# A matmul kernel whose hand-written opening list is written anew, with sixteen idle matmuls of the identity in it

## The chip, the cores and the metric

The kernel runs on one core of a Trainium2 chip. The metric is the device time of one launch in microseconds (us); less is better. The kernel before took 530.66, 531.22 and 532.54 us in three runs, median 531.22 us.

## The reference

Two stages follow each other. The first is a recurrence over 768 tokens for 4 batches and 8 heads of 48 channels; the second is a gated feed-forward layer on the 3072 resulting rows of 384.

```python
for t in range(S):
    kt, vt, rt = (k[:, :, t], v[:, :, t], r[:, :, t])
    cur = np.einsum('bhd,bhe->bhde', u[None] * kt, vt)
    y[:, :, t] = np.einsum('bhd,bhde->bhe', rt, state + cur)
    state = w[None, :, :, None] * state + np.einsum('bhd,bhe->bhde', kt, vt)
...
gate = 1.0 / (1.0 + np.exp(-(x @ w_gate)))
val = x @ w_val
return (gate * val @ w_out).astype(np.float32)
```

## The kernel before, in words

The recurrence is cut into 12 chunks of 64 tokens, and each chunk into two groups of heads: 24 groups n. For a group, TensorE makes a table of scores (step Z, line 375), VectorE copies its lower triangle into a zeroed tile (K, line 383), TensorE multiplies that with the values and the queries with the running state (I, line 337) and forms the state's increment (O, line 337 too). ScalarE decays the state (d) and VectorE adds the increment (s). The result is split into a rounded high part (h, ScalarE, line 474) and a low rest (l, VectorE, line 478); both are the rows that the feed-forward layer reads.

The feed-forward layer runs on six tiles of 512 rows with the 1536 inner columns in 12 blocks f. A block's up-projection U is 18 matmuls (line 516): nine for the gate half into one accumulator bank, nine for the value half into another. Then follow a sigmoid (g, ScalarE), a product (m, VectorE), a rounded copy (H, ScalarE), its rest (q) and the down-projection D (line 554). Weights arrive in 64-bit words, and are cast (c), joined (j), rounded (w) and left with a rest (o, or ov on VectorE) before U can use them. For the first row tile the blocks f = 0 and f = 1 run on 256 rows at a time, since its second chunk is ready only later.

Every engine works its instructions off in the order in which they were written. For the first row tile that order is a string, START, of step names: "Z.2" is the score step of group 2, "u.0a" the gate half of block 0 on the first 256 rows. A second, regular loop does the other five tiles. The kernel uses eight accumulator banks: two for scores (sc), three in a rotating pool (ring), three that hold the down-projection's sums (acc0 to acc2). Early on, acc0 also takes four transpositions (step tt, line 197). The identity is made first on GpSimd (masks.py:197 and masks.py:199).

In the working below, "value half" and "gate half" are the two halves of U; the first blocks are U.0 (f = 0) and U.1 (f = 1) on the first 256 rows.

Of the kernel before, what the change touches and what calls it, by code (L numbers as in the profile page):

```python
# [21 lines left out]
P = 128  # L22
# [21 lines left out]
L.0 W.0 L.1 X.0 W.1 L.2 X.1 X.2 tc A.0 tk ti.1 R.0 ti.0 k.0 tp tr Z.0 tt K.0 I.0 c0.0 A.1 c0.1 tn  # L44
h.0 c.1 T.2 T.1 k.1 Rv.1 j0.1 l.0 Tv.0 j0.0 Z.1 O.0 W.2 F.0 W.3 L.3 L.4 W.4 X.3 j.1 K.1 I.1 O.1 A.2
w0.0 sa.0 w.1 h.1 w0.1 o0.1 o.1 R.3 Rv.2 k.2 o0v.0 l.1 s.1 Z.2 K.2 U.0 I.2 O.2 g.0 c.2 d.2 A.3 m.0
U.1 H.0 g.1 h.2 j.2 k.3 s.2 l.2 q.0 T.3 m.1 F.2 L.5 W.8 X.4 L.6 W.5 W.6 L.7 X.5 F.1 X.6 L.8 W.7 Z.3
K.3 I.3 O.3 w.2 A.4 k.4 H.1 c.3 h.3 l.3 R.4 D.0 Z.4 U.2 d.3 s.3 g.2 c.4 j.3 w.3 j.4 qv.1 m.2 o.2
U.4 H.2 g.4 w.4 A.5 K.4 q.2 U.3 D.2 g.3 Rv.5 m.3 k.5 ov.3 m.4 T.4 I.4 O.4 Z.5 H.3 A.6 d.4 h.4 H.4
c.6 c.5 k.6 s.4 K.5 l.4 Tv.5 j.6 R.6 q.3 D.1 D.3 U.5 I.5 g.5 h.5 j.5 qv.4 l.5 m.5 o.4 Z.6 D.4 R.7  # L50
O.5 U.6 A.7 d.5 H.5 K.6 k.7 s.5 q.5 T.6 w.5 ov.5 U.7 c.8 c.7 g.6 j.7 m.6 L.9 X.8 ub Y.8 W.9 W.10
X.7 I.6 Z.7 O.6 D.5 w.6 g.7 ov.6 d.6 w.7 H.6 s.6 j.8 qv.6 h.6 l.6 m.7 w.8 ov.7 H.7 qv.7 D.6 U.8 K.7
R.8 c.9 ov.8 g.8 m.8 Tv.7 H.8 U.9 qv.8 g.9 k.8 j.9 w.9 o.9 m.9 D.7 U.10 g.10 H.9 c.10 j.10 m.10 q.9
D.8 I.7 H.10 d.7 Z.8 O.7 h.7 w.10 D.9 s.7 U.11 ov.10 l.7 W.11 F.5 X.9 F.6 F.3 F.7 F.4 Y.9 qv.10
g.11 c.11 j.11 D.10 U.12 m.11 w.11 R.9 ov.11 U.13 g.12 H.11 qv.11 m.12 H.12 qv.12 g.13 t.8 D.11 b.8
i.8 D.12 K.8 k.9 m.13 H.13 q.13 b.9 T.9 t.9 i.9 T.8
# [4 lines left out]
def rwkv_then_moe(ctx: ExitStack, tc: tile.TileContext, wd, ub, ch, tk, rt, wt, rk0, vn0, wd0, out):  # L61
# [38 lines left out]
    def load_channels(n):  # L100
        c, g = GROUPS[n]
        chan[n] = ach.tile([P, 2, 512], F32, name="chan")
        nc.sync.dma_start(out=chan[n], in_=ch[c, g])

    def load_tokens(n):
        c, g = GROUPS[n]
        toks[n] = atk.tile([P, 2, TKW], F32, name="toks")
        nc.sync.dma_start(out=toks[n], in_=tk[c, g])
# [15 lines left out]
    def constants():  # L124
        make_identity(nc, ident)
        nc.gpsimd.memset(causal, 0.0)
# [7 lines left out]
        for t in score:  # L134
            nc.gpsimd.memset(t, 0.0)
        nc.gpsimd.memset(state, 0.0)
        nc.scalar.activation(table, ident[:, 0:1], AF.Sigmoid)
        nc.vector.memset(tops[0].rearrange("q n two -> q (n two)").bitcast(F32), 0.0)
        nc.gpsimd.memset(tops[1].rearrange("q n two -> q (n two)").bitcast(F32), 0.0)


# [109 lines left out]
    def round_weights(f, c):  # L251
# [3 lines left out]
        nc.scalar.copy(out=whi[f][:, c], in_=w32[f][:, c])  # L255
# [24 lines left out]
    def table_of(n):  # L280
        return tabk[:, 4 * GROUPS[n][1] : 4 * GROUPS[n][1] + 4]
# [8 lines left out]

    def queries(n, eng=nc.gpsimd):
# [210 lines left out]
    class Moe:  # L502
# [3 lines left out]

        def up(self, f):
            w = whi[f], wlo[f]
            self.pair[f] = []
            for g in range(2):  # L510
                o = one_bank()
                self.pair[f].append(o)
                k = 0
                for kt in range(3):
                    for a, b in PASS:
                        nc.tensor.matmul(  # L516
                            o[:, self.cols], w[a][:, g * DM + kt * P : g * DM + (kt + 1) * P],
                            self.x[:, kt, b, self.cols], start=(k == 0), stop=(k == 8),
                        )
                        k += 1  # L520
# [106 lines left out]
    steps = {
        "b": own_tokens, "i": diagonal, "ub": lambda: load_bonus(),
        "N": idle_matmuls,
        "L": load_channels, "X": load_tokens, "Y": load_own, "W": load_weights, "A": bonus_keys, "R": queries, "t": turn_queries,  # L630
        "k": keys, "T": token_keys, "Z": scores, "K": keep, "I": apply, "O": outer,
        "d": decay_state, "s": add_state, "h": x_high, "l": x_low, "F": fills, "D": finish,
        "tc": constants, "tk": channel_table, "ti": inverses, "tp": token_powers,
        "tr": lambda: token_order(nc.vector.tensor_copy), "trA": lambda: token_order(nc.scalar.copy),
        "sa": lambda n: add_state(n, nc.scalar.copy), "tt": token_turn, "tn": token_table,
        "c": lambda f: cast_top(f, ALL), "c0": lambda j: cast_top(0, HALVES[j]),
        "j": lambda f: join_words(f, ALL), "j0": lambda j: join_words(0, HALVES[j]),
        "w": lambda f: round_weights(f, ALL), "w0": lambda j: round_weights(0, HALVES[j]),
        "o": lambda f: rest_of_weights(f, ALL), "o0": lambda j: rest_of_weights(0, HALVES[j]),
# [3 lines left out]
        "qv": lambda i: moe_of(items[i]).h_low(items[i][2], nc.vector),  # L643
        "U": lambda i: moe_of(items[i]).up(items[i][2]),
        "g": lambda i: moe_of(items[i]).sigmoid(items[i][2]),
        "m": lambda i: moe_of(items[i]).product(items[i][2]),
        "H": lambda i: moe_of(items[i]).h_high(items[i][2]),
        "q": lambda i: moe_of(items[i]).h_low(items[i][2]),
# [25 lines left out]
    for i in range(n0, len(items)):  # L674
# [24 lines left out]
        finish(i - 1)  # L699
# [193 lines left out]
```

## Time and profile before

| | us |
|---|---|
| Runs, median (lowest to highest) | 531.22 (530.66 to 532.54) |
| Span of the profiled execution, first to last instruction | 532.9 |
| TensorE busy in it | 510.4 |
| TensorE's first instruction at | 7.63 |
| VectorE, ScalarE, GpSimd busy | 203.4, 186.9, 189.9 |

The page gives no other time of the profiled execution than its span. A busy time is the sum of an engine's stretches of work; the span less that is what the engine stood idle. Stretches of a row in time order begin at the first number and last for the second, and a bracket at the end holds the idle time ahead and what ended it.

### The profile page before, as it was taken

To read this page: it belongs to the slowest core of one execution; us is meant where nothing else is said; L and a number is where in the kernel's file an instruction comes from. 1 tells how busy PE (TensorE), PEld (TensorE's weight loads), DVE (VectorE), ACT (ScalarE), POOL (GpSimd) and SP (SyncE) were. 2 spreads that over 40 slices of the span, in tenths; PEclk is the share of its full clock that TensorE was granted. 3 is DMA by queue.
4 is the path that set the end of the run, shared out by engine and by line. 5 is a ranking of instruction groups with operands and counts; after the bars stand their busy time and mean duration, and the time that the engine had idled before them with its cause. 6 is when DMAs were issued, how large, how long until landed. Compare 5 with 4: busy or idle time off the path is not lost. (4 is left out here: it accounts for less than half of the span.)

```text
span 532.9 us, 11951 instructions
## 1 busy us (share of the span) xinstructions
PE 510.4 (96%) x5204; PEld 424.4 (80%) x5204; DVE 203.4 (38%) x344; ACT 186.9 (35%) x396; POOL 189.9 (36%) x159
## 2 busy tenths in 40 slices
PE   3689999999999999999999999999999999999994
PEld 3678878888888888888888888888888888888883
DVE  8857868464243242341431532431442211111111
ACT  5577665545133233233232331331432222212111
POOL 4362530406453352443452552542253111112210
PEclk9999999999999999999999999999999999999999
DMA  8939736030321230420221420312400000100001
GB/s 321 366 111 352 301 112 284 4 103 21 127 87 26 71 106 1 145 86 17 80 61 48 145 87 0 97 34 72 146 17 2 11 11 10 60 0 1 0 2 64
DMA packets 15723, 47.84 MB, mean 90 GB/s; under 512 B 2384, under 2 KB 5200, under 8 KB 14256
## 3 DMA queue, kind: packets, MB, share of 16 engines
q1 hardware_dynamic: 15664, 47.01, 25.3%
q8 instruction: 43, 0.70, 0.6%
q14 instruction: 16, 0.13, 0.1%
HBM read 39.92 MB, written 4.72 MB: 84 GB/s over the span
## 5 line engine op out<-in xcount | busy, mean ns | idle before, releaser
L516 PE MATMUL ring<-xt,wx 128*128 128x512 f32 (+1 forms) x1332 | 309.9, 387 | 0.9 <-ACT sg L525 0.5
L516 PEld LDWEIGHTS ring<-xt,wx 128*128 128x128 f32 x1332 | 247.8, 191 | 51.3 <-ACT sg L525 0.7
L538 POOL TENSOR_TENSOR h<-sg,h 128x512 fp32r<-128x512 f32 (+1 forms) x66 | 88.5, 1340 | 259.5 <-ACT h L534 259.5
L554 PE MATMUL acc<-h,wx 128*128 128x512 f32 (+1 forms) x666 | 161.6, 388 | 0.4 <-POOLq L714 0.4
L554 PEld LDWEIGHTS acc<-h,wx 128*128 128x128 f32 x666 | 121.2, 188 | 25.6 <-POOLq L714 0.8
L529 DVE TENSOR_TENSOR sg<-ring,sg 128x512 f32<-128x512 f32 (+1 forms) x74 | 50.0, 676 | 237.0 <-PE ring L516 235.6
L525 ACT ACTIVATE sg<-ring 128x512 f32<-128x512 f32 (+1 forms) x74 | 43.4, 586 | 157.4 <-PE ring L516 157.4
L534 ACT CAST h<-sg 128x512 fp32r<-128x512 f32 (+1 forms) x74 | 45.0, 608 | 144.2 <-DVE sg L529 138.2
L293 POOL TENSOR_TENSOR dec<-chan,tabk 128x512 f32<-128x512 f32 x21 | 29.0, 1381 | 12.5 <-PE ring L337 12.4
L478 DVE TENSOR_TENSOR xt<-ring,xt 112x256 fp32r<-112x256 f32 (+1 forms) x52 | 19.9, 418 | 33.1 <-ACT xt L474 33.0
L308 POOL TENSOR_TENSOR toks<-toks,tabn 128x384 f32<-128x384 f32 x19 | 24.0, 1267 | 13.7 <-DMA toks<-in_tk 13.7
L314 POOL TENSOR_TENSOR dec<-dec,toks 128x384 f32<-128x384 f32 x16 | 16.3, 1020 | 27.3 <-DMA dec<-in_rt 27.3
L304 DVE TENSOR_TENSOR chan<-chan,tabk 128x512 f32<-128x512 f32 x24 | 25.0, 1042 | 0.9 <-ACT dec L287 0.9
L375 PE MATMUL sc<-dec,chan 48*64 48x64 f32 x768 | 17.4, 231 | 7.7 <-DVE chan L304 7.6
L383 DVE COPY_PREDICATED score<-masks,sc 128x512 f32<-128x512 int32 x32 | 23.9, 747 | 1.9 <-PE sc L375 1.1
L428 ACT ACTIVATE state<-state,pw 112x96 f32<-112x96 f32 x80 | 23.4, 362 | 2.6 <-PE ring L337 2.6
L337 PE MATMUL ring<-score,toks 64*48 64x64 f32 (+1 forms) x768 | 17.2, 230 | 5.0 <-DVE score L383 4.1
L447 DVE TENSOR_TENSOR state<-state,ring 48x192 f32<-48x192 f32 (+1 forms) x52 | 17.9, 350 | 9.7 <-ACT xt L474 4.7
L375 PEld LDWEIGHTS sc<-dec,chan 48*64 48x64 f32 x768 | 15.0, 145 | 8.1 <-POOL dec L293 7.6
L247 DVE SCALAR_TENSOR_TENSOR wf<-wr,top 128x1152 int32<-128x1152 int32 (+1 forms) x13 | 16.9, 1310 | 9.4 <-ACT top L240 5.7
L337 PEld LDWEIGHTS ring<-score,toks 64*48 64x48 f32 (+1 forms) x768 | 14.6, 137 | 6.4 <-DVE score L383 4.8
L474 ACT CAST xt<-ring 112x256 fp32r<-112x256 f32 (+1 forms) x52 | 16.7, 364 | 7.6 <-PE ring L337 7.3
(60 smaller groups left out, 250.5 us busy)
## 6 DMA issues: line engine op xcount, KB each, us to landing
wr<-in_wt SPq DMA_DIRECT2D x11, 1152.0 KB, 9.2
chan<-in_ch SPq DMA_DIRECT2D x24, 512.0 KB, 4.2
toks<-in_tk SPq DMA_DIRECT2D x24, 400.0 KB, 4.8
out_y<-wf SPq DMA_DIRECT2D x17, 256.0 KB, 2.5
dec<-in_rt SPq DMA_DIRECT2D x16, 192.0 KB, 2.7
xt<-xt SPq DMA_DIRECT2D x30, 64.0 KB, 2.3
wr<-in_wt SPq DMA_DIRECT2D x2, 576.0 KB, 5.4
xt<-xt SPq DMA_DIRECT2D x12, 32.0 KB, 4.2
```

Of the source, the lines that this page charges most:

```text
L293: eng.tensor_tensor(v4(t[:, 0]), v4(chan[n][:, 0]), bc2(table_of(n)[:, :, ::-1]), ALU.mult)
L304: nc.vector.tensor_tensor(v4(k), v4(k), bc2(table_of(n)), ALU.mult)
L308: eng.tensor_tensor(v4(k), v4(k), bc2(tabn[:, 4 * g : 4 * g + 4]), ALU.mult)
L337: nc.tensor.matmul(yb[n][bank][64 * half : 64 * half + m, cs], lhsT, rhs, start=first, stop=stop, skip_group_check=True,)
L375: nc.tensor.matmul(sc[64 * gm : 64 * gm + 64, be, o : o + C], kk[row, cs : cs + C], rr[row, cs : cs + C], start=True, stop=True,)
L383: nc.vector.copy_predicated(t.rearrange("q (b m i) -> q b m i", b=2, m=4), masks[:, m].bitcast(I32).unsqueeze(1).unsqueeze(1).broadcast_to ...
L516: nc.tensor.matmul(o[:, self.cols], w[a][:, g * DM + kt * P : g * DM + (kt + 1) * P], self.x[:, kt, b, self.cols], start=(k == 0), stop=(k ...
L525: nc.scalar.activation(sg[:, c], self.pair[f][0][:, c], AF.Sigmoid, scale=UP)
L529: nc.vector.tensor_tensor(sg[:, c], self.pair.pop(f)[1][:, c], sg[:, c], ALU.mult)
L534: nc.scalar.copy(out=h[:, 0, c], in_=sg[:, c])
L538: eng.tensor_tensor(h[:, 1, c], self.sg.pop(f)[:, c], h[:, 0, c], ALU.subtract)
L554: nc.tensor.matmul(self.acc[d][:, self.cols], w[a][:, 2 * DM + d * P : 2 * DM + (d + 1) * P], h[:, b, self.cols], start=(f == 0 and k == 0 ...
```

## The change

START is written anew. The steps got finer names (a block's gate half u and value half v apart; making the identity, the masks and the zeroed tiles apart), and the string names a few steps in another sequence. As the instructions stand on each engine, this leaves SyncE and GpSimd without any difference, ScalarE with two pairs of neighbours exchanged later on (a rounded copy of h and one of weights), and VectorE with none but a tile's name. TensorE gets idle matmuls: step "N.k" multiplies the identity by itself k times, 128 by 128 in fp32, into the first accumulator bank, and nothing reads the result. There are sixteen at eight places: six ahead of Z.0, two behind I.0, two behind O.0, one behind O.1, two behind Z.2, one between the halves of U.1, one behind Z.3 and one behind O.3. Beside them, the output banks of group 1 come from acc1 and acc2 in place of the rotating three.

```diff
-    def idle_matmuls(k):
-        t = pacc.tile([P, 512], F32, name="acc2")
+        t = accs[0][0] if 0 in accs else pacc.tile([P, 512], F32, name="acc0")
         for _ in range(k):
             nc.tensor.matmul(t[:, 0:P], ident, ident, start=True, stop=True)
...
     def outputs(n):
-        yb[n] = one_bank(), one_bank()
+        if n == 1:
+            yb[n] = tuple(pacc.tile([P, 512], F32, name=f"acc{i}") for i in (1, 2))
+        else:
+            yb[n] = one_bank(), one_bank()
...
-L.0 W.0 L.1 X.0 W.1 L.2 X.1 X.2 tc A.0 tk ti.1 R.0 ti.0 k.0 tp tr Z.0 tt K.0 I.0 c0.0 A.1 c0.1 tn
+ta L.0 tov.0 tc tb W.0 ts.0 L.1 ts.1 X.0 tz W.1 tk L.2 X.1 to.1 N.6 ti.1 X.2 ti.0 A.0 R.0 W.2 k.0
+c0.0 tp tr Z.0 tt A.1 K.0 c0.1 tn k.1 I.0 Rv.1 N.2 j0.1 h.0 l.0 Tv.0 Z.1 c.1 j0.0 O.0 A.2 j.1 w0.0
...
+        def up_one(self, f, g):
+            w, o, k = (whi[f], wlo[f]), one_bank(), 0
+            self.pair.setdefault(f, []).append(o)
+            for kt in range(3):
+                for a, b in PASS:
+                    nc.tensor.matmul(
+                        o[:, self.cols], w[a][:, g * DM + kt * P : g * DM + (kt + 1) * P],
+                        self.x[:, kt, b, self.cols], start=(k == 0), stop=(k == 8),
+                    )
+                    k += 1
```

On TensorE the program begins, before, with the scores of group 0 (sc) and the four transpositions (acc from sg):

```order
L888 UNCONDITIONAL_BRANCH
L375 MATMUL sc<-dec,chan 64x64 x16
L375 MATMUL sc<-chan,dec 64x64 x16
L197 MATMUL acc_201<-spare,sg 128x128 x4
L337 MATMUL ring<-score_97,toks 64x64 x2
```

After the change six idle matmuls (acc from spare, the identity) stand ahead of them:

```order
L921 UNCONDITIONAL_BRANCH
L640 MATMUL acc_151<-spare 128x128 x6
L392 MATMUL sc<-dec,chan 64x64 x16
L392 MATMUL sc<-chan,dec 64x64 x16
L204 MATMUL acc_211<-spare,sg 128x128 x4
L351 MATMUL ring<-score_97,toks 64x64 x2
```

The lines of the kernel shifted (375 is now 392, and so on), and only the six rows are new. Farther on, on TensorE again, before, O.1 ends, then come the scores of group 2 and the 18 matmuls of U.0:

```order
L337 MATMUL ring<-toks 48x48 x2
L375 MATMUL sc<-dec,chan 64x64 x16
L375 MATMUL sc<-chan,dec 64x64 x16
L516 MATMUL ring<-xt,wx 128x256 x18
L337 MATMUL ring<-dec,state 64x64 x2
```

After, one idle matmul stands between O.1 and Z.2 and two between Z.2 and U.0, and O.1 writes to acc1 and acc2:

```order
L351 MATMUL acc_337<-toks 48x48
L351 MATMUL acc_336<-toks 48x48
L640 MATMUL acc_378<-spare 128x128
L392 MATMUL sc<-dec,chan 64x64 x16
L392 MATMUL sc<-chan,dec 64x64 x16
L640 MATMUL acc_420<-spare 128x128 x2
L529 MATMUL ring<-xt,wx 128x256 x18
L351 MATMUL ring<-dec,state 64x64 x2
```

Nothing else moved there. At U.1 and Z.3, before:

```order
L516 MATMUL ring<-xt,wx 128x256 x18
L375 MATMUL sc<-dec,chan 64x64 x16
L375 MATMUL sc<-chan,dec 64x64 x16
L337 MATMUL ring<-dec,state 64x64 x2
```

and after, with one idle matmul between the halves of U.1 and one behind Z.3:

```order
L529 MATMUL ring<-xt,wx 128x256 x9
L640 MATMUL acc_432<-spare 128x128
L529 MATMUL ring<-xt,wx 128x256 x9
L392 MATMUL sc<-dec,chan 64x64 x16
L392 MATMUL sc<-chan,dec 64x64 x16
L640 MATMUL acc_432<-spare 128x128
L351 MATMUL ring<-dec,state 64x64 x2
```

Again the rows between stand as they stood.

## Rows read from the trace of the kernel before

**Rows 1.** The page's first line.

```profile
span 532.9 us, 11951 instructions
```

**Rows 2.** Stretches: length, busy us of each engine (count), granted clock, DMA share.

```profile
0.00:40.00 40.00, 25.53 (x624) 23.08 (x625) 29.34 (x52) 23.49 (x53) 19.57 (x26) 1.00 0.71 266
40.00:100.00 60.00, 58.80 (x830) 49.12 (x832) 43.90 (x61) 37.77 (x70) 18.66 (x12) 1.00 0.60 233
100.00:500.00 400.00, 400.00 (x3656) 331.24 (x3645) 126.32 (x226) 119.81 (x265) 146.43 (x118) 1.00 0.18 56
531.60:532.90 1.30, 0.00 (x0) 0.00 (x0) 0.00 (x0) 0.00 (x0) 0.00 (x0) 0.50 0.03 6
```

**Rows 3.** Instructions in time order, TensorE: start, length, what, idle ahead.

```profile
7.63 1.13 PE L375 MATMUL sc<-dec,chan 48*64 48x64 f32 x32 [7.63 <-DVE chan L304]
...
11.31 1.12 PE L337 MATMUL ring<-score,toks 64*64 64x64 f32 x32 [0.65 <-DVE score L383]
...
17.63 1.12 PE L337 MATMUL ring<-score,toks 64*64 64x64 f32 x32 [2.24 <-DVE score L383]
20.45 0.99 PE L337 MATMUL ring<-toks 64*64 64x48 f32 x30 [1.71 <-POOL toks L308]
...
23.21 0.79 PE L516 MATMUL ring<-xt,wx 128*128 128x256 f32 x2
24.18 3.78 PE L516 MATMUL ring<-xt,wx 128*128 128x256 f32 x16 [0.18 <-DVE xt L478]
27.90 1.12 PE L337 MATMUL ring<-dec,state 48*64 48x64 f32 x32
...
31.18 2.24 PE L516 MATMUL ring<-xt,wx 128*128 128x256 f32 x9
33.89 1.33 PE L516 MATMUL ring<-xt,wx 128*128 128x256 f32 x9 [0.47 <-ACT sg L525]
35.15 0.69 PE L375 MATMUL sc<-dec,chan 48*64 48x64 f32 x32
...
36.14 0.64 PE L337 MATMUL ring<-dec,state 48*64 48x64 f32 x32
37.96 0.68 PE L337 MATMUL ring<-score,toks 64*64 64x64 f32 x32 [1.19 <-DVE score L383]
38.46 0.64 PE L337 MATMUL ring<-toks 64*48 64x48 f32 x32
```

**Rows 4.** Instructions of line 197: ns min/median/max, first and last start us.

```profile
L197 PE MATMUL acc<-spare,sg x4: 421/421/473, 9.5 to 10.2; 128*128 128x128 f32 x4
```

**Rows 5.** Instructions in time order, GpSimd.

```profile
1.03 0.29 POOL masks.py:199 TENSOR_SCALAR_AFFINE_SELECT spare<-spare 128x128 f32<-128x128 f32 x1
...
17.94 2.46 POOL L308 TENSOR_TENSOR toks<-toks,tabn 128x384 f32<-128x384 f32 x2 [10.95 <-DMA toks<-in_tk]
23.91 4.03 POOL L258 TENSOR_TENSOR wx<-wf,wx 128x576 fp32r<-128x576 f32 x2 [3.52 <-ACT wx L255]
```

**Rows 6.** Instructions in time order, ScalarE.

```profile
21.62 1.51 ACT L474 CAST xt<-ring 48x256 fp32r<-48x256 f32 x4 [3.77 <-PE ring L337]
...
26.08 0.39 ACT L525 ACTIVATE sg<-ring 128x256 f32<-128x256 f32 x1 [2.25 <-PE ring L516]
26.36 1.52 ACT L240 ACTIVATE top<-wr 128x1152 f16<-128x1152 bf16 x1
28.70 1.17 ACT L428 ACTIVATE state<-state,pw 112x96 f32<-112x96 f32 x4 [0.82 <-PE ring L337]
29.77 1.26 ACT L287 ACTIVATE dec<-chan,wu 128x128 f32<-128x128 f32 x4
...
33.45 0.38 ACT L525 ACTIVATE sg<-ring 128x256 f32<-128x256 f32 x1 [2.12 <-PE ring L516]
```

**Rows 7.** Instructions in time order, VectorE.

```profile
16.09 1.48 DVE L383 COPY_PREDICATED score<-masks,sc 128x512 f32<-128x512 int32 x2
...
22.40 1.73 DVE L478 TENSOR_TENSOR xt<-ring,xt 48x256 fp32r<-48x256 f32 x4 [1.39 <-ACT xt L474]
```

More of the change, by code (lines that the diff above doesn't have):

```diff
@@ L98, in rwkv_then_moe, with load_channels, load_tokens @@
     chan, toks = {}, {}
[L100 removed]
+    def load_channels(n, eng=nc.sync):
         c, g = GROUPS[n]
         chan[n] = ach.tile([P, 2, 512], F32, name="chan")
[L103 to L105 removed]
+        eng.dma_start(out=chan[n], in_=ch[c, g])
+    def load_tokens(n, eng=nc.sync):
         c, g = GROUPS[n]
         toks[n] = atk.tile([P, 2, TKW], F32, name="toks")
[L108 removed]
+        eng.dma_start(out=toks[n], in_=tk[c, g])
     def load_own(n):
@@ L122, in rwkv_then_moe, with identity, causal_masks @@
     table = const.tile([P, 1], F32, name="table")
-    def constants():
+    def identity():
         make_identity(nc, ident)
+    def causal_masks():
         nc.gpsimd.memset(causal, 0.0)
@@ L133, in constants, with clear_scores, clear_state, first_table @@
             nc.gpsimd.tensor_copy(masks[lo : lo + 64, 1], ident[lo : lo + 64, lo : lo + 64])
-        for t in score:
-            nc.gpsimd.memset(t, 0.0)
-        nc.gpsimd.memset(state, 0.0)
+    def clear_scores(i, eng=nc.gpsimd):
+        eng.memset(score[i], 0.0)
+    def clear_state(eng=nc.gpsimd):
+        eng.memset(state, 0.0)
+    def first_table():
         nc.scalar.activation(table, ident[:, 0:1], AF.Sigmoid)
-        nc.vector.memset(tops[0].rearrange("q n two -> q (n two)").bitcast(F32), 0.0)
-        nc.gpsimd.memset(tops[1].rearrange("q n two -> q (n two)").bitcast(F32), 0.0)
+    def clear_top(i, eng=nc.gpsimd):
+        eng.memset(tops[i].rearrange("q n two -> q (n two)").bitcast(F32), 0.0)
     pw = const.tile([P, N2, 97], F32, name="pw")
@@ L232, in load_weights @@
             a, b = 4 * c.start, 4 * c.stop
-            nc.sync.dma_start(out=t[:, 1 + a : 1 + b], in_=wt[f, :, c].bitcast(U16))
+            eng.dma_start(out=t[:, 1 + a : 1 + b], in_=wt[f, :, c].bitcast(U16))
     def cast_top(f, c):
@@ L249, in join_words, with round_weights @@
         )
-    def round_weights(f, c):
+    def round_weights(f, c, copy=nc.scalar.copy):
         if f not in wparts:
@@ L254, in round_weights @@
             whi[f], wlo[f] = wparts[f][:, 0:W3], wparts[f][:, W3 : 2 * W3]
-        nc.scalar.copy(out=whi[f][:, c], in_=w32[f][:, c])
+        copy(out=whi[f][:, c], in_=w32[f][:, c])
     def rest_of_weights(f, c, eng=nc.gpsimd):
@@ L470, in x_of, with x_high @@
         ]
-    def x_high(n):
+    def x_high(n, copy=nc.scalar.copy):
         for x, y in x_of(n, 0):
-            nc.scalar.copy(out=x, in_=y)
+            copy(out=x, in_=y)
     def x_low(n):
@@ L485, in fill, with fills @@
             )
-    def fills(n):
+    def fills(n, eng=nc.sync):
         c, g = GROUPS[n]
@@ L505, in __init__ @@
             self.pair, self.sg, self.h = {}, {}, {}
-        def up(self, f):
[L508 to L520, printed above, removed]
+        def up_one(self, f, g):
[6 more added lines that the diff above has]
+                        self.x[:, kt, b, self.cols], start=(k == 0), stop=(k == 8),
+                    )
+                    k += 1
+        def up(self, f):
+            self.up_one(f, 0)
+            self.up_one(f, 1)
         def sigmoid(self, f):
@@ L592, in store_last @@
             nc.sync.dma_start(out=out[2 * P : 3 * P, c + i], in_=o)
-    halves = [(0, g) for g in range(HALF)] + [(1, g) for g in range(HALF)] + [(2, g) for g in range(HALF, NF)]
-    items = [(0, h, f) for h, f in halves]
-    n0 = len(items)
+    items = [(0, 2, NF - 1)]
     for ti in range(1, len(TILES)):
@@ L609, in moe_of, with finish @@
         return moes[ti, h]
-    def finish(i):
-        ti, h, f = items[i]
-        moe_of(items[i]).down(f)
+    def finish(it):
+        ti, h, f = it
+        moe_of(it).down(f)
         if f == NF - 1:
@@ L622, in idle_matmuls @@
     def idle_matmuls(k):
-        t = pacc.tile([P, 512], F32, name="acc2")
+        t = accs[0][0] if 0 in accs else pacc.tile([P, 512], F32, name="acc0")
         for _ in range(k):
             nc.tensor.matmul(t[:, 0:P], ident, ident, start=True, stop=True)
+    V, G, AC = nc.vector, nc.gpsimd, nc.scalar
     steps = {
+        "ta": identity, "tb": causal_masks, "tc": first_table,
+        "ts": clear_scores, "tsv": lambda i: clear_scores(i, V), "tz": lambda: clear_state(), "tzv": lambda: clear_state(V),
+        "to": clear_top, "tov": lambda i: clear_top(i, V),
         "b": own_tokens, "i": diagonal, "ub": lambda: load_bonus(),
         "N": idle_matmuls,
[L630 to L633, printed above, removed]
+        "L": load_channels, "X": load_tokens, "Y": load_own, "W": load_weights,
+        "La": lambda n: load_channels(n, AC), "Xa": lambda n: load_tokens(n, AC), "Wa": lambda f: load_weights(f, AC),
+        "Lp": lambda n: load_channels(n, G), "Xp": lambda n: load_tokens(n, G), "Wp": lambda f: load_weights(f, G),
+        "A": bonus_keys, "Av": lambda n: bonus_keys_on(n, V), "Ap": lambda n: bonus_keys_on(n, G),
+        "R": queries, "t": turn_queries,
+        "k": keys, "kp": lambda n: keys(n, G), "T": token_keys, "Z": scores, "K": keep, "I": apply, "O": outer,
+        "d": decay_state, "s": add_state, "h": x_high, "hv": lambda n: x_high(n, V.tensor_copy), "l": x_low,
+        "F": fills, "Fa": lambda n: fills(n, AC), "Fp": lambda n: fills(n, G),
+        "tk": channel_table, "ti": inverses, "tp": token_powers,
         "tr": lambda: token_order(nc.vector.tensor_copy), "trA": lambda: token_order(nc.scalar.copy),
+        "trp": lambda: token_order(G.tensor_copy),
         "sa": lambda n: add_state(n, nc.scalar.copy), "tt": token_turn, "tn": token_table,
@@ L642, in rwkv_then_moe, with block @@
         "Rv": lambda n: queries(n, nc.vector), "Tv": lambda n: token_keys(n, nc.vector),
[L643 to L648, printed above, removed]
+    }
+    def block(arg):
+        return (0, "ab".index(arg[-1]), int(arg[:-1])) if arg[-1] in "ab" else (0, 2, int(arg))
+    moe_steps = {
+        "U": Moe.up, "u": lambda m, f: m.up_one(f, 0), "v": lambda m, f: m.up_one(f, 1), "g": Moe.sigmoid, "m": Moe.product, "H": Moe.h_high, "q": Moe.h_low,
+        "qv": lambda m, f: m.h_low(f, nc.vector),
     }
@@ L651, in rwkv_then_moe @@
         name, _, arg = step.partition(".")
-        steps[name](*([int(arg)] if arg else []))
+        if name == "D":
+            finish(block(arg))
+        elif name in moe_steps:
+            moe_steps[name](moe_of(block(arg)), block(arg)[2])
+        else:
+            steps[name](*([int(arg)] if arg else []))
     def load(n):
@@ L673, in rwkv_then_moe @@
     load(n + 2)
-    for i in range(n0, len(items)):
+    for i in range(1, len(items)):
         ti, h, f = items[i]
```

50 lines of the change are left out of this document (28 added, 22 removed).

## The prediction, made before the changed kernel ran

> **What bounds the kernel now.** I read the table of stretches first. From 100 to 500 us TensorE is busy for all 400 us, from 40 to 100 for 58.8 of 60, from 0 to 40 for only 25.5 [rows 2]. So the kernel is bound by TensorE from about 40 us on, and what an edit of the opening is worth is how much earlier TensorE leaves it: every us gained there moves the rest forward, as long as the others keep up. Of the span of 532.9 us [rows 1] the opening holds 14.5 us of idle.
>
> Next, TensorE in time order, for two things. First its waits: 7.63 us to the first scores, 2.24 ahead of I.1, 1.71 ahead of O.1, 0.47 between the halves of U.1, 1.19 ahead of I.3 [rows 3]. Second, the speed of equal work. The nine matmuls of U.1's gate half take 2.24 us, the nine of its value half 1.33, with nothing but a pause of 0.47 between them [rows 3]; that is 249 and 148 ns each. All TensorE work ahead of that point is slow in the same way: I.1 of 32 small instructions takes 1.12 us, I.3 gives way to O.3 after 0.50 (37.96 to 38.46). [...] By the durations the array ran on the lower level until about 33.5 us, and rose after TensorE had worked from 20.45 on with no pause longer than half a microsecond.
>
> **The change part by part.** SyncE, GpSimd and VectorE issue the same in the same order; ScalarE's two exchanged pairs lie far behind, where TensorE is always busy: 0, bounds ±0.4 (a sigmoid of 0.38, [rows 6], the nearest step of that engine). Group 1's outputs in acc1 and acc2 must be read before D.0 writes there; the last reader in question is l.1, done at 24.13 [rows 7], and D.0 comes behind O.3 at about 39 [rows 3]: 0. In return U.0 no longer asks for group 1's banks; it did not wait for them: 0.
>
> An idle matmul. The trace has no such instruction. The nearest is the transposition of the same 128x128 fp32 shape: four starting from 9.5 to 10.2, 0.23 us apart [rows 4]. A plain fp32 matmul leaves two instructions in this trace (the 16 of a score block show as x32, [rows 3]), so I take 2 x 0.23 = 0.46 us on the lower level and half, 0.23, on the upper. Bounds: one transposition, 0.23 (0.12), and two that do not overlap, 2 x 0.42 = 0.84 (0.42). Below nothing the issue of one cannot go; what it may give back is the clock, counted below.
>
> Where they lie, on the lower level:
> 1. Six ahead of Z.0. The identity is ready at 1.32 [rows 5]; 6 x 0.46 = 2.8 ends near 4.1, and Z.0 waits for VectorE until 7.63: hidden (with 0.84 each still done at 6.4).
> 2. Two behind I.0, two behind O.0, 0.92 each. I.1 waits until 17.63 for the copy of its scores on VectorE, which starts at 16.09 behind other work there [rows 7]; TensorE had 2.24 to spare against 1.84: hidden.
> 3. One behind O.1 and two behind Z.2: on the path, 1.38, less the 0.18 that U.0 stands waiting for l.1 [rows 3], since it now starts near 24.5: +1.2.
> 4. One in U.1: U.1's value half goes into the bank that the sigmoid must first read, 0.47 of wait: hidden. One behind Z.3: under the 1.19 ahead of I.3: hidden. One behind O.3: on the path, +0.23 on the upper level.
>
> What the clock gives. With the fills, TensorE works from 20.45 to the end of U.0 without the stall ahead of U.0's third matmul; and from 11.31 to about 17.2 instead of 15.4 (17.63 less the wait of 2.24, [rows 3]). My forecast (E) is that the clock has risen by Z.2. Then O.1, from 20.45 (held by GpSimd's two steps, 17.94 + 2.46, [rows 5], which wait for a DMA) lasts 0.5; idle 0.23; Z.2 1.0 (35.15 to 36.14, [rows 3]); idle 0.46: TensorE reaches U.0 at 22.65. h.1 follows O.1 and ends 0.55 sooner, near 22.6, l.1 near 23.55 instead of 24.13 [rows 6, 7]; the third matmul waits for it. Gate half: 23.55 + 7 x 0.148 = 24.6; value half, which needs the first third of GpSimd's 4.03 on the weights' rest (begun 0.6 sooner, done near 24.65), 25.95 instead of 27.90. Now ScalarE sets the pace: sigmoid g.0 from 24.7, 0.4; cast c.2 1.5 to 26.6; decay d.2 1.2 to 27.8; A.3 1.25 to 29.05; H.0 0.35, g.1 0.4 to 29.8 [rows 6]. U.1's gate half is done by then (weights' rest at 27.35 + 1.33 = 28.7), so its value half runs from 29.8 to 31.1, against 35.15 before: 4.0 sooner. Behind it the whole chain, K.3, I.3, O.3, the fills and the loads that SyncE issues after them, starts from these steps and shifts along. Sum: -4.0 + 0.23 = -3.8, with bounds -3.2 (idle matmuls at 0.84) and -4.1.
>
> The profiled span is 532.9, the nearest run 532.54, both above the median by 1.3 to 1.7. I set the profile beside that run: 532.54 - 3.8 = **528.7 us**. Set against the median it would be 527.4, which goes into the range.
>
> **The rivals.**
>
> M, the rise comes only in the middle of U.0. For it speaks that between 15.4 and 20.45 there is little work but I.1 even with two more idle matmuls, so a clock that had risen at 15 may be down again, and that U.0 was still slow in the trace. U.0 starts at 24.5; say four matmuls at 0.236 (3.78 / 16) and the rest at 0.148: gate half done 26.2, value half 27.55, g.0 to 26.75, c.2 to 28.25, d.2 29.4, A.3 30.65, H.0 and g.1 31.4, value half of U.1 to 32.75: 2.4 sooner, less 0.23: 532.54 - 2.2 = 530.3. [...]
>
> S, slower: the rise does not come sooner. Place: O.1 to U.0, three idle matmuls on the path at the lower level. U.0 and all behind it is late by 1.2 until the rise; if that stays at 33.5, half of the delay is won back by work that then runs fast (+0.6), if it moves along, none (+1.2); with the idle matmul behind O.3: +0.8 to +1.4, and about +2.5 at 0.84 each. 532.54 + 1.1 = 533.6. It decides as soon as the identity's matmuls count for less than real ones to whatever raises the clock, or U.0's rise hangs on U work alone. Against it: the stretch before the rise held small matmuls as well as nine of U.1.
>
> G, given back: the clock rises early, but from 40 to 60 us the transfers are the limit and TensorE waits there. For it: 1.2 us of idle from 40 to 100 and a DMA share of 0.60 [rows 2]. Against it: the DMAs are issued by steps that shift too. If half of E's 3.8 is kept, 532.54 - 1.9 = 530.6.
>
> [...]
>
> **How the numbers follow.** E 0.45, M 0.33, S 0.14, G 0.08. A change under 0.3% (1.6 us) can't be told from none here: faster is below 529.6, slower above 532.8. E is faster for 0.41 of its 0.45; M for 0.05, else the same; G the same or a trace of faster; S slower but for 0.01. Faster 0.47, same 0.40, slower 0.13. The range runs from 527.0 (E against the median, with a little more) to 531.3 (M with idle matmuls at their upper bound, and G); S is left out.
>
> **What would show it.** Right: U.0's 18 matmuls near 0.148 us each, its end near 26, U.1's value half ending near 31, I.3 near 33.7. M: U.0 begins slow and ends fast, U.1 ends near 32.8. S: U.0 slow throughout, starting at 24.5. Twelve instructions of 128x128 ahead of Z.0, from 1.4 on and 0.23 apart, would confirm an idle matmul's price. Wrong altogether: Z.0 or I.1 later than 7.63 and 17.63, since then the fills were not hidden, or a TensorE wait between 40 and 100 us that is new.

## The result and the profile after

The change made the kernel slower: 534.8 us in the median of 20 runs, against 532.06 for 20 runs of the kernel before beside them; ratio 1.0054, 95% interval 1.0038 to 1.0070. I had forecast 528.7, with a range from 527.0 to 531.3. The profiled execution took 534.83 us with a span of 533.1, so about 1.7 us lie around the span. That also places the profile that I had read: its span of 532.9 [rows 1] belongs, by this estimate, to a run of about 534.6, above every one of the 20 runs (530.38 to 533.84). I had set it beside a run of 532.54. Such executions of the kernel before do occur: beside three of the four later sets of experiments its slowest run took 534.88, 535.33 and 535.30.

TensorE's opening after the change, in time order (start, length, what, idle ahead; L640 are the idle matmuls, L392 the scores, L351 I and O, L529 is U):

```profile
1.38 2.93 PE L640 MATMUL acc<-spare 128*128 128x128 f32 x12 [1.38 <-POOL spare masks.py:199]
7.64 1.13 PE L392 MATMUL sc<-dec,chan 48*64 48x64 f32 x32 [3.33 <-DVE chan L318]
...
16.24 1.22 PE L640 MATMUL acc<-spare 128*128 128x128 f32 x4
17.62 1.36 PE L351 MATMUL acc<-score,toks 64*64 64x64 f32 x32 [0.16 <-DVE score L400]
20.44 1.09 PE L351 MATMUL acc<-toks 64*64 64x48 f32 x32 [1.46 <-POOL toks L322]
21.47 0.79 PE L640 MATMUL acc<-spare 128*128 128x128 f32 x2
22.19 1.13 PE L392 MATMUL sc<-dec,chan 48*64 48x64 f32 x32
23.10 1.08 PE L392 MATMUL sc<-chan,dec 48*64 48x64 f32 x32
24.11 1.22 PE L640 MATMUL acc<-spare 128*128 128x128 f32 x4
24.98 3.27 PE L529 MATMUL ring<-xt,wx 128*128 128x256 f32 x18
28.18 0.68 PE L351 MATMUL ring<-dec,state 48*64 48x64 f32 x32
...
30.22 1.34 PE L529 MATMUL ring<-xt,wx 128*128 128x256 f32 x9
...
32.03 1.33 PE L529 MATMUL ring<-xt,wx 128*128 128x256 f32 x9 [0.25 <-ACT sg L542]
```

The hidden places are hidden: Z.0 and I.1 start where they did [rows 3], at 7.64 and 17.62. The three idle matmuls on the path show in the rows at 21.47 and 24.11 (each leaves two instructions). U.0 starts at 24.98 instead of 23.21, begins slow and ends fast (3.27 us for 18, between 18 x 0.148 = 2.66 and the 4.6 it took). U.1's value half starts at 32.03 instead of 33.89: 1.86 us sooner than in the profile before. This is rival M's picture, about half a us later than M had it (U.1 ends at 33.3, not 32.8). The gain does not reach the end, as three new waits of TensorE from 60 us on show (engine, what it did, what it waited for; us in total, times, longest); in the profile before no wait from 60 us on was longer than 0.4:

```profile
PE ring L529 <- DVE xt L495: 1.1, 1, 1.1
PE sc L392 <- issue: 0.8, 1, 0.8
PE acc L571 <- ACT h L551: 0.5, 1, 0.5
```

Two of the three lie between 40 and 100 us (61.9 and 79.1), where the prediction had named a new wait as a sign that it was wrong altogether. The table of stretches says the same: beside the 400.00 of before [rows 2], TensorE is no longer always busy from 100 us on.

```profile
0.00:40.00 40.00, 31.85 (x723) 28.50 (x724) 31.74 (x56) 25.14 (x58) 19.75 (x26) 1.00 0.71 268
40.00:100.00 60.00, 58.13 (x842) 48.82 (x841) 40.50 (x57) 37.08 (x69) 18.24 (x13) 1.00 0.59 232
100.00:500.00 400.00, 398.89 (x3568) 329.79 (x3562) 126.51 (x226) 118.74 (x261) 144.75 (x117) 1.00 0.18 56
```

### The profile page after: what moved, and what is told of

It reads as the page before. It is cut to its first block, busy times and chain, and to the rows that moved or that the text cites. A ratio compares the mean times of both kernels' runs of the same rounds, so it can differ in the third digit from the quotient of the medians.

```text
span 533.1 us, 12014 instructions
## 1 busy us (share of the span) xinstructions
PE 515.2 (97%) x5236; PEld 428.2 (80%) x5236; DVE 202.6 (38%) x344; ACT 186.8 (35%) x396; POOL 188.2 (35%) x159
## 5 line engine op out<-in xcount | busy, mean ns | idle before, releaser
L529 PE MATMUL ring<-xt,wx 128*128 128x512 f32 (+1 forms) x1332 | 307.4, 385 | 1.4 <-DVE xt L495 1.1
L529 PEld LDWEIGHTS ring<-xt,wx 128*128 128x128 f32 x1332 | 246.0, 189 | 51.1 <-issue 1.5
L307 POOL TENSOR_TENSOR dec<-chan,tabk 128x512 f32<-128x512 f32 x21 | 27.7, 1318 | 15.8 <-PE ring L351 15.7
L495 DVE TENSOR_TENSOR xt<-ring,xt 112x256 fp32r<-112x256 f32 (+1 forms) x48 | 18.3, 419 | 31.4 <-ACT xt L491 31.4
L464 DVE TENSOR_TENSOR state<-state,ring 48x192 f32<-48x192 f32 (+1 forms) x52 | 17.9, 350 | 9.5 <-PE ring L351 5.9
L392 PE MATMUL sc<-dec,chan 48*64 48x64 f32 x768 | 17.2, 231 | 3.3 <-DVE chan L318 3.3
L254 DVE SCALAR_TENSOR_TENSOR wf<-wr,top 128x1152 int32<-128x1152 int32 (+1 forms) x13 | 16.2, 1261 | 8.0 <-ACT top L247 6.3
L265 POOL TENSOR_TENSOR wx<-wf,wx 128x1152 fp32r<-128x1152 f32 (+1 forms) x5 | 12.1, 2420 | 18.8 <-ACT wx L262 18.8
L247 ACT ACTIVATE top<-wr 128x1152 f16<-128x1152 bf16 (+1 forms) x13 | 18.2, 1420 | 0.5 <-DMA wr<-in_wt 0.5
L392 PEld LDWEIGHTS sc<-dec,chan 48*64 48x64 f32 x768 | 14.8, 145 | 4.3 <-POOL dec L307 3.6
L351 PE MATMUL ring<-score,toks 64*48 64x64 f32 (+1 forms) x736 | 15.6, 222 | 2.2 <-DVE score L400 1.3
```

Source lines behind the costliest of these rows:

```text
L307: eng.tensor_tensor(v4(t[:, 0]), v4(chan[n][:, 0]), bc2(table_of(n)[:, :, ::-1]), ALU.mult)
L392: nc.tensor.matmul(sc[64 * gm : 64 * gm + 64, be, o : o + C], kk[row, cs : cs + C], rr[row, cs : cs + C], start=True, stop=True,)
L529: nc.tensor.matmul(o[:, self.cols], w[a][:, g * DM + kt * P : g * DM + (kt + 1) * P], self.x[:, kt, b, self.cols], start=(k == 0), stop=(k ...
```

## The experiments

Times are medians of 12 runs each (six for the kernel with 34 idle matmuls), in rounds with the kernel before; ratios are to that kernel. To place a loss more finely than runs that scatter over 1.5 to 7 us can, I compare when the same matmul of U and D, counted from 0 in each trace, starts in two traces: between two such matmuls the traces repeat to 0.05 us where nothing waits (4.57 to 4.60 us from matmul 190 to 210, in the kernels with the old order there). From matmul 310 to the last of them, 417.67 us, thirteen of the fourteen traces agree (one takes 417.89), so what is lost ahead of matmul 310 lasts to the end.

**ScalarE's exchanged pairs, and the idle matmuls, apart.** Two edits in START, alone and together:

```diff
-X.7 w.7 s.6 W.11 X.9 D.3 H.4 j.8 h.6
+X.7 w.7 W.11 X.9 D.3 H.4 s.6 j.8 h.6
...
-h.7 s.7 D.7 b.8 w.10 u.9
+h.7 D.7 b.8 w.10 s.7 u.9
```

> The changed kernel with its sixteen idle matmuls, but with ScalarE's two exchanged pairs put back (the state copy of group 6 behind the rounded h again, that of group 7 behind the rounded weights). Theory A: the exchanged pairs make TensorE wait (0.45 at 79 us, 1.1 at 104.5 us in the changed kernel's trace); without them these two waits are gone and the time falls by 1.3 to 1.9 us, to about 533.2 against 534.8. Theory B: the loss is the idle matmuls and the clock in the opening; the time stays at 534.8 and the waits at 79 and 104.5 us turn up elsewhere.

> The changed kernel without its sixteen idle matmuls, exchanged pairs kept. Theory A: still slower than before by what the pairs cost, 1.3 to 1.9 us, about 533.7. Theory B: as before the change, 532.1. If the idle matmuls do gain in the opening (the changed profile left the opening 1.9 us sooner than the one before), it is slower than the changed kernel.

> The changed kernel without the idle matmuls and with the exchanged pairs put back: every engine then works in the order of before, and only group 1's output banks differ. Theories A and B alike: 532.1, within 0.1% of before. If it is slower, the banks or something not seen in the order cost time.

> The kernel before itself, for the spread of its times and a second trace of it. Ratio 1.000. If the moment at which the clock rises varies between executions, the trace shows the rise at another time than the 33 us of the first, and U.0 and U.1 end sooner with an earlier rise.

| | us | ratio [95%] |
|---|---|---|
| changed kernel | 534.8 | 1.0054 [1.0038, 1.0070] |
| pairs put back (idle matmuls kept) | 533.03 | 1.0022 [1.0002, 1.0042] |
| idle matmuls out (pairs kept) | 533.20 | 1.0006 [0.9988, 1.0025] |
| both | 531.93 | 0.9992 [0.9976, 1.0008] |
| kernel before, as a run of its own | 531.28 | 0.9987 [0.9971, 1.0003] |

The first row is the result above. Neither theory alone: by the medians the pairs cost 1.3 us and the idle matmuls 1.1, and with both undone the loss is gone, so group 1's banks cost nothing that can be measured. How the loss divides can't be taken from the times: the kernel before, as a run of its own, lies 1.1 us below its own median in the same rounds (532.37). The traces divide it, and there the pairs are seen directly. ScalarE near 101 us, before: high rows of group 7 (L474), weights (L255), then the state copy (L453), which needs VectorE's sum.

```profile
101.42 0.65 ACT L474 CAST xt<-ring 112x256 fp32r<-112x256 f32 x2
101.96 1.17 ACT L255 CAST wx<-wf 128x1152 fp32r<-128x1152 f32 x1
103.02 0.71 ACT L453 COPY state<-spare 48x192 f32<-48x192 f32 x2
```

The same three after the change; the copy comes second, waits 0.93, and the weights wait behind it.

```profile
100.22 0.65 ACT L491 CAST xt<-ring 112x256 fp32r<-112x256 f32 x2
101.80 0.71 ACT L470 COPY state<-spare 48x192 f32<-48x192 f32 x2 [0.93 <-DVE spare L464]
102.53 1.16 ACT L262 CAST wx<-wf 128x1152 fp32r<-128x1152 f32 x1
```

And VectorE after the change: the weights' rest (L265) waits for them, the low rows of group 7 (L495) come behind it, and U.9's value half waits for them: they are the last reader of a bank that it wants.

```profile
103.72 1.36 DVE L265 TENSOR_TENSOR wx<-wf,wx 128x1152 fp32r<-128x1152 f32 x1 [2.00 <-ACT wx L262]
104.99 0.75 DVE L495 TENSOR_TENSOR xt<-ring,xt 112x256 fp32r<-112x256 f32 x2
```

TensorE at the two places, before, where it does not wait:

```profile
78.25 4.39 PE L554 MATMUL acc<-h,wx 128*128 128x512 f32 x18
...
103.45 4.24 PE L516 MATMUL ring<-xt,wx 128*128 128x512 f32 x18
```

and after the change:

```profile
79.10 2.34 PE L571 MATMUL acc<-h,wx 128*128 128x512 f32 x9 [0.45 <-ACT h L551]
...
105.56 2.32 PE L529 MATMUL ring<-xt,wx 128*128 128x512 f32 x9 [1.11 <-DVE xt L495]
```

From matmul 190 to 210 of U and D, TensorE takes 4.57 to 4.60 us in the kernels with the pairs put back and 5.31 in both with them exchanged; from 290 to 310 it takes 4.53, against 5.57 (idle matmuls out) and 5.92 (changed). So the pairs cost 0.7 + 1.0 to 1.4 us of TensorE's time.

**One pair alone.** The edit is the second of the two above, on the kernel with both undone.

> No idle matmuls, and of ScalarE's two exchanged pairs only the second: the state copy of group 7 ahead of the rounding of block 10's weights. If the exchange holds the weights' rest, the low rows of group 7 and so the bank of U.9's value half, TensorE loses 1.0 to 1.4 us near 104 us (the stretch from matmul 290 to 310 of U and D takes 5.6 to 5.9 in place of 4.53) and nothing near 79 us; the time is about 1 us (0.2%) above the kernel with neither.

532.16 us, ratio 1.0000 [0.9975, 1.0026]; the runs can't tell it from none. In its trace the stretch at 104 us takes 5.57 in place of 4.53, and the one at 79 us 4.60 as without. The 1.04 us are there, and the total of a single pair is too small for twelve runs. The path is not quite the one that I had named. Here, as with the idle matmuls out and both pairs kept, the low rows are late too (102.35), but the wait ends with the sigmoid of U.9's gate half:

```profile
102.56 2.33 PE L529 MATMUL ring<-xt,wx 128*128 128x512 f32 x9 [0.75 <-ACT sg L542]
```

Why U.9's value half waits for the sigmoid in these two kernels and for the low rows in the changed one was not followed; that the exchange brings a wait at this place is shown, its last link only for the changed kernel.

**The second trace of the kernel before.** It differs from the first: U.0 starts at 21.70, and U.1's gate half is fast.

```profile
21.70 4.63 PE L516 MATMUL ring<-xt,wx 128*128 128x256 f32 x18
26.27 1.12 PE L337 MATMUL ring<-dec,state 48*64 48x64 f32 x32
...
28.74 1.34 PE L516 MATMUL ring<-xt,wx 128*128 128x256 f32 x9
30.55 1.33 PE L516 MATMUL ring<-xt,wx 128*128 128x256 f32 x9 [0.47 <-ACT sg L525]
```

U.1's value half starts at 30.55, not 33.89 [rows 3]. This execution took 530.19 us, the fastest of its twelve, but the three other kernels without idle matmuls agree with it: 30.50 (idle matmuls out), 31.03 (both undone) and 31.27 (one pair). The profile that I had read was a late one, by 2.6 to 3.4 us. With idle matmuls the value half starts at 32.03 (changed) and 32.54 (pairs put back): against these four the sixteen lose 0.8 to 2.0 us here, where against my profile they had seemed to gain.

Against this second trace the whole loss can be laid out. In the changed kernel U.1's value half starts 1.48 us later; from matmul 135 to 150 it takes 1.09 more, from 190 to 210 0.71, from 290 to 310 1.39; behind U.1 it gains back 0.14. The last matmul of U and D starts 4.50 us later. The two executions lie 4.64 apart (534.83 and 530.19), the medians only 2.7, so a usual pair of executions differs by less than this list.

The trace with the pairs put back also shows the two levels of the clock, upper and lower, in its granted-clock column: 1.00 from 4.4 to 7.6, behind the six idle matmuls, while TensorE rests (0.00 us busy), 0.50 from 7.8 to 28.1, and 1.00 again from 28.3 on. At 0.50 the halves of Z.2 take 1.13 and 1.08 us, at 1.00 those of Z.3 0.69 and 0.65. Where the column reads 1.00 in an opening it is not enough by itself: it does so in the changed kernel too (the row from 0 to 40 us above), where Z.0 takes 1.13 and 1.10 us. So a level is read from the durations as well, and that the six idle matmuls raised the clock is not shown.

```profile
4.40:7.60 3.20, 0.00 (x0) 0.01 (x1) 3.20 (x5) 2.13 (x5) 2.49 (x3) 1.00 1.01 403
7.80:28.10 20.30, 18.10 (x353) 16.16 (x351) 16.39 (x28) 10.63 (x24) 6.85 (x5) 0.50 0.98 383
```

**A stall inside a score block.** In both kernels with sixteen idle matmuls TensorE stops inside a score block of group 6, for 0.77 and 1.30 us, "issue": nothing that the profile shows. Here with the pairs put back:

```profile
61.04 0.64 PE L392 MATMUL sc<-chan,dec 48*64 48x64 f32 x29
62.97 0.33 PE L392 MATMUL sc<-chan,dec 48*64 48x64 f32 x3 [1.30 <-issue]
```

The first matmul behind it is number 1105 of all of TensorE's, counted from 0, in both, and a packet of 16 KB on the instruction queue ends 1.3 us ahead of it in both. My theory I: TensorE's instructions come in such blocks, and a block that ends in a run of small matmuls (about 16 ns each) is used up before the next is there. The 16 ns are measured (32 in 0.50 us, [rows 3]); the rest is a theory.

> ScalarE's order of before, and of the sixteen idle matmuls only the three on the path: one behind O.1, two behind Z.2. Theory P (the price of the opening is these three): U.0 begins about 1.4 us after O.1 and Z.2 alone would let it, as with all sixteen, and 0.5 to 1.2 us of that last to the end, 0.1 to 0.2% slower than before. Theory I (the rest of the loss is the stall of TensorE for nothing that the profile shows, 0.8 and 1.3 us inside a score block near 61.5 us, seen in both kernels with sixteen idle matmuls, and set by how many instructions stand ahead): no such stall here, as only 3 instead of 16 are ahead.

> ScalarE's order of before, and sixteen idle matmuls again, but all where TensorE waits anyway: twelve ahead of Z.0, two behind I.0, two behind O.0; none from O.1 on. Theory P: the opening is as without idle matmuls (U.0 begins 0.0 to 0.2 us later), and the time is that of before. Theory I: the stall near 61.5 us is there again, 0.8 to 1.3 us, since the same number of instructions stands ahead of it, and the time is about 1 us (0.2%) above that of the kernel without idle matmuls, although none is on the path.

> ScalarE's order of before, and eight idle matmuls where TensorE waits anyway: six ahead of Z.0, two behind O.0. Theory I (the stall near 61.5 us is TensorE's instructions arriving late, and comes when the count of instructions ahead puts the end of a delivered block into a run of small matmuls): with eight instead of sixteen ahead, the end falls into the 128x512 matmuls of D.1 and U.3, and there is no stall; 531.5 to 532.5, as before. A rival, that idle matmuls ahead of Z.0 cost by themselves (through the clock that rises and falls again): about 533, and the stall of 0.8 to 1.3 us is there.

Of the sixteen, the first kept only the three on the path (N.1 behind O.1, N.2 behind Z.2), the second had N.12, N.2, N.2 ahead of Z.0 and behind I.0 and O.0, the third N.6 and N.2 ahead of Z.0 and behind O.0. With sixteen, all where TensorE waits anyway, the stall is there, ahead of matmul 1104:

```profile
60.10 0.64 PE L392 MATMUL sc<-chan,dec 48*64 48x64 f32 x28
61.76 0.33 PE L392 MATMUL sc<-chan,dec 48*64 48x64 f32 x4 [1.02 <-issue]
```

With eight, three or none it is not. From matmul 135 to 150 of U and D TensorE takes 6.00 us in these (6.61 in the first trace of before, where it waits for a sigmoid) and 7.09 to 7.61 in the three with sixteen. Theory I's forecast came out for this stall: in these kernels it came with the number of instructions ahead, not with their place (1.02 us with all sixteen hidden). The traces show a packet's end 1.3 us ahead of it in the first two; that a block of TensorE's instructions ends at that matmul is my estimate from the count. A second place fits it: ahead of matmul 221, inside I.1, TensorE stops for 0.79 and 0.73 us in the two kernels with an exchanged pair and no idle matmuls, and there too a packet ends 1.5 us ahead (at 18.0 and 17.9). In the three other traces without idle matmuls that packet ends at 15.9 to 17.3, and TensorE does not stop there. The times: three 531.73, ratio 0.9999 [0.9979, 1.0020]; sixteen hidden 533.10, 1.0015 [0.9989, 1.0041]; eight hidden 532.67, 1.0020 [0.9995, 1.0046]. The intervals of all three hold 1, so the runs don't tell them from before. Theory P fails for the three on the path: U.0 starts at 23.28, later than 22.24 without (both undone), but the clock rises while it runs (granted 0.50 from 18.3 to 25.0 us, 0.68 in the mean from 20 to 28; 18 matmuls in 3.20 us), and U.1's value half starts at 30.25 against 31.03.

```profile
18.30:25.00 6.70, 6.53 (x120) 6.04 (x117) 5.89 (x11) 2.14 (x5) 3.07 (x3) 0.50 0.90 308
```

One trace does not show that the three brought the rise forward. The eight hidden ones are not free as expected: their U.0 starts at 23.21, since O.1 waited until 20.46, and U.1's value half at 32.18; with sixteen hidden it starts at 31.59. So the half is late in both kernels that have no idle matmul on the path, and not in the one that has only those.

**Forecast E itself.** 34 idle matmuls that fill TensorE's waits: N.14 ahead of Z.0, six behind the transpositions, N.2, N.6, N.3 behind I.0, O.0 and I.1, N.1 behind Z.2, in U.1 and behind Z.3.

> ScalarE's order of before, and 34 idle matmuls that fill TensorE's waits from 1.4 to 20 us: 14 ahead of Z.0, 6 behind the transpositions (into acc2), 2 behind I.0, 6 behind O.0, 3 behind I.1, 1 behind Z.2, 1 in U.1, 1 behind Z.3. It tests forecast E itself: if the clock rises near 4 to 8 us and these keep it up, U.0 runs at 0.148 us a matmul from its first one, U.1's value half ends 2 us or more sooner than without, and the time falls by 1.5 to 3.5 us below before. If the clock falls back in between, or does not rise, it is 0.5 to 3 us slower than before.

```profile
22.58 0.50 PE L529 MATMUL ring<-xt,wx 128*128 128x256 f32 x2
23.58 2.17 PE L529 MATMUL ring<-xt,wx 128*128 128x256 f32 x16 [0.49 <-DVE xt L495]
...
29.75 1.33 PE L529 MATMUL ring<-xt,wx 128*128 128x256 f32 x9 [0.25 <-ACT sg L542]
...
49.44 0.64 PE L392 MATMUL sc<-chan,dec 48*64 48x64 f32 x28
54.01 0.37 PE L392 MATMUL sc<-chan,dec 48*64 48x64 f32 x2 [3.93 <-issue]
```

The clock is kept (granted 1.00 from 4.6 to 52.2 us, Z.0's halves in 0.69 and 0.68), and the opening runs nearly as I had worked it out: U.0 from 22.58 (22.65), U.1's value half from 29.75 (29.8). The last link was another, though: ScalarE waited 0.32 us for U.1's gate half, where I had ScalarE set the pace, so agreement to 0.05 us is in part luck. And the time is 536.49, ratio 1.0088 [1.0058, 1.0119], slower against an expected gain: with 68 instructions more ahead, TensorE stops inside a score block at 50 us, for 3.93 us (by theory I the end of another block), with the clock at 0.50 behind it (52.4 to 59.1). The transfers were full then (DMA share 0.99 from 48 to 52 us), and the packet itself began only at 51.7; that the full queue made this stall the longest agrees with these figures but was not varied.

```profile
52.40:59.10 6.70, 5.09 (x22) 4.85 (x22) 2.96 (x6) 2.47 (x3) 1.04 (x1) 0.50 0.65 237
```

So I gave each idle matmul four times the work, 128x512 with the identity four times on the moving side: three ahead of Z.0, one behind the transpositions, three behind O.0, two behind I.1, and a narrow one behind Z.3.

```diff
+            nc.tensor.matmul(
+                t.rearrange("q (m x) -> q m x", m=4), ident,
+                ident.unsqueeze(1).broadcast_to([P, 4, P]), start=True, stop=True,
+            )
```

> ScalarE's order of before, and nine idle matmuls of 128x512 (the identity four times as the moving side), each with the work of four and the instructions of one: 3 ahead of Z.0, 1 behind the transpositions, 3 behind O.0, 2 behind I.1, and one narrow one behind Z.3. Forecast E with its stall taken away: if the clock rises near 4 to 8 us and is kept, U.0 begins fast near 22 us and U.1's value half by 29.8 as in the kernel with 34 (29.75), there is no stall for instructions up to 65 us, and the time is 0.5 to 2.5 us below before (529.5 to 531.5). If the clock falls back, or the tokens land late and O.1 stays at 20.3, it is 532 to 534.

531.28, ratio 0.9981 [0.9956, 1.0005]: inside the range that I had named for success, but not told from before, and not by that way. No stall at 50 or 61 us, and the granted clock is 1.00 from 5.4 to 500 us (Z.0's halves in 0.69 and 0.68, U.0's last sixteen in 2.21); but I.1 stopped for 1.13 us on "issue" (matmul 221 again), and the two behind it held O.1 back, so that U.1's value half starts at 30.64 and not 29.8.

```profile
17.39 0.44 PE L351 MATMUL acc<-score,toks 64*64 64x64 f32 x11
18.96 0.54 PE L351 MATMUL acc<-score,toks 64*64 64x64 f32 x21 [1.13 <-issue]
19.43 1.98 PE L645 MATMUL acc<-spare 128*128 128x512 f32 x4
21.35 0.61 PE L351 MATMUL acc<-toks 64*64 64x48 f32 x30
...
30.64 1.33 PE L529 MATMUL ring<-xt,wx 128*128 128x256 f32 x9 [0.47 <-ACT sg L542]
```

Without the two behind I.1, twice the same kernel:

> As the kernel with nine wide idle matmuls, but without the two behind I.1, which in its trace held O.1 back from 19.5 to 21.35. If the clock, up since about 5 us, outlives the wait ahead of O.1, U.0 begins near 21.8 and ends near 25, U.1's value half begins near 29 instead of 30.6, and the time is 529 to 530.5, 0.2 to 0.5% below before. If it falls in that wait, U.0 is slow and the time is that of before, 531.5 to 532.5.

> The same kernel a second time, since a difference of 0.2 to 0.4% is about what twelve runs can tell from none: the same time, and a second trace of whether the clock is kept.

531.73 and 531.45, ratios 1.0001 [0.9979, 1.0024] and 1.0007 [0.9984, 1.0030]: no gain. In one trace the clock fell ahead of U.0, by its durations (two matmuls in 0.80 us and sixteen in 3.78, behind a Z.2 half of 0.68), after a wait of 1.87 us for the tokens, and U.1's value half starts at 31.62; in the other it outlived one of 1.44 (0.50 and 2.19), and the half starts at 29.64. O.1 and the value half in the one and in the other:

```profile
20.33 0.61 PE L351 MATMUL acc<-toks 64*64 64x48 f32 x30 [1.87 <-POOL toks L322]
...
31.62 1.33 PE L529 MATMUL ring<-xt,wx 128*128 128x256 f32 x9 [0.47 <-ACT sg L542]
```

```profile
20.39 0.67 PE L351 MATMUL acc<-toks 64*64 64x48 f32 x32 [1.44 <-POOL toks L322]
...
29.64 1.33 PE L529 MATMUL ring<-xt,wx 128*128 128x256 f32 x9 [0.47 <-ACT sg L542]
```

No version beat the kernel before by more than can be told from none.

## Why the prediction was wrong

**The step that failed first** is "ScalarE's two exchanged pairs lie far behind, where TensorE is always busy: 0, bounds ±0.4". That TensorE never waits there in the old order says nothing of a new one: I had bounded the exchange by a step's own length, not by the wait that the state copy brings in front of its neighbour. I did not follow who stands behind it. Measured: 0.7 us at 79 and 1.0 to 1.4 at 104 us, in the changed kernel 2.1 of the 4.5 us laid out above. That the exchange brings these waits is shown in the traces, by undoing both pairs and by one pair alone; the times of twelve runs can't show a single pair.

**The condition of E failed.** "The clock has risen by Z.2" was false in the changed kernel: U.0 began slow at 24.98. In a sister kernel with the same opening, the one with the pairs put back, the granted clock was 1.00 from 4.4 to 7.6 us and 0.50 from 7.8 to 28.1, and Z.0, from 7.62 on, took 1.12 and 1.15 us. In the kernel with 34 idle matmuls, where the condition held, the sum was right to 0.1 us (29.75 against 29.8, in part by luck), but its worth was not. Nor was a clock once up always kept over the pause ahead of O.1, as E needs: in one of the two runs with seven wide idle matmuls it fell behind a wait of 1.87 us (sixteen matmuls of U.0 in 3.78 us, against 2.19 in the other).

**The base of the sum was one late execution.** E's 4.0 us were counted against a value half at 33.89. In the other trace of the kernel before it starts at 30.55, and in the three other kernels without idle matmuls at 30.50 to 31.27, so E held a gain of 0.7 to 1.5 us against these and not 4.0. The two traces of before differ in the moment of the rise, by the durations: U.1's gate half is slow in one (2.24 us) and fast in the other (1.34). The base of the sum took the moment of one of them as the kernel's. The two also differ ahead of that, O.1 starting at 20.45 in one and 18.68 in the other, so not all of the 3 us need be the clock. That the profile's span lay above all three runs was the sign.

From 528.7 to 534.8 are 6.1 us. By the traces about 2.1 of them are the run that I had set the profile beside (532.54 in place of about 534.6), 1.9 the opening's gain (1.86 in place of 3.8), and 2.1 the pairs (0.7 and 1.4 against the profile that I had read).

**A term was missing.** Sixteen idle matmuls are also 32 more matmuls in TensorE's stream, and with them came the stall of 0.77 us in a score block, with 1.1 us lost there in all against the second trace of before (0.5 against the first, which had waits of its own there). That they moved the end of a block of instructions there is theory I, which the runs agree with. I had priced an idle matmul by its time alone.

**Right:** its price, 12 instructions in 2.93 us, 0.49 for each idle matmul against 0.46. For the upper level the sum took half, 0.23, which no row of before shows; the kernel with 34 shows twelve instructions in 1.50 us there, 0.25 each. Right too: that the first ten and those in U.1 and behind Z.3 are hidden from TensorE's own steps; U.0's start near 24.5 (24.98). Rival S had the side, but its mechanism is not borne out. The opening does lose 1.5 us by U.1's value half against the other trace of before (32.03 against 30.55), near S's 1.2; but the three idle matmuls on the path, by themselves, did not make the half late (30.25), and kernels with none there have it late (31.59 and 32.18). What the late ones share is an O.1 from 20.3 us on and a U.0 that starts slow. And the larger part of the loss came later. Rival G, given back between 40 and 60 us by transfers, is not what happened: it was given back at 61, 79 and 104 us, and not by data.

**Open:** why O.1 starts at 20.3 to 20.5 in some traces and at 18.6 to 19.6 in others. GpSimd's token step, which it waits for, starts at 17.5 to 17.9 or at 16.2 to 16.7. In all fourteen traces the late start goes with a first 16 KB instruction packet at 12.9 to 15.6 us, the early one with 16.1 to 17.0. Of the eight traces with idle matmuls ahead of Z.0 seven have the late start, of the six without only one, the profile that I had read. So much of what the opening lost may be this, and not the idle matmuls' own time. That the packet delays the tokens agrees with it; it was not varied by itself, so it is not shown.

## What to carry to other kernels

Before a change's gain is counted against one profile, hold that profile's time against the runs: if it lies at their edge, its waits are not the usual ones. When two neighbours on an engine are exchanged, ask what the one moved ahead waits for and who stands behind, even where the busiest engine never waits today. Ask what filler costs in instructions as well as in time: here the kernels with sixteen narrow idle matmuls stood still for 0.77 to 1.30 us near 61 us, and those with seven or nine wide ones and one narrow did not stop there (the one with nine did inside I.1, for 1.13 us).

## What was not expected of the hardware

- TensorE stopped inside runs of small matmuls (about 16 ns each) with nothing in the profile that it waited for: for 0.77, 1.30 and 1.02 us near 61 us in the three kernels with sixteen idle matmuls, and for 3.93 us at 50 us in the one with 34, where the transfers were full too (DMA share 0.99); inside I.1 for 0.73 to 1.13 us in three others. The kernels with eight, three and none did not stop near 61 us. That TensorE outran its instructions is my theory I, not a row of the profile.
- The clock went up and fell again within an opening. With twelve idle matmuls ahead of Z.0 its halves took 0.69 and 0.68 us, and the granted clock was 0.50 from 10.7 to 27.6 us. In two runs of one kernel, with waits of 1.87 and 1.44 us ahead of O.1, it fell in one (sixteen matmuls of U.0 in 3.78 us) and was kept in the other (2.19). Two runs do not show that the wait's length decided it.
- 128x512 idle matmuls gave the same cover with fewer instructions: ahead of Z.0 three of them, six instructions, took 4.51 to 5.17 us, and fourteen of 128x128, 28 instructions, 4.88. In one of three traces with them the granted clock stayed at 1.00 (5.4 to 500 us); in the other two it fell once and rose again, by the durations: U.0's last sixteen took 3.78 us and U.1's gate half 1.33, or I.0 took 1.04 us and Z.1's first half 0.64.
